# Gathered rows of experts 2 to 7: through a scratch in DRAM and VectorE's 32x32 turn, in place of transposes on TensorE

## The chip, the cores and the metric

The kernel runs on one core of one Trainium2 chip. The metric is the device time of one execution in microseconds, taken as the median of the runs.

## The reference, cut to what matters

Three stages follow each other: attention on 4 x 576 tokens with 8 heads (local or strided masks), a dense feed-forward block on 2304 tokens of 512 elements, and a mixture of 8 experts, of which each token visits two. The change is in the third stage:

```
noisy_logits = x @ w_gate + log1p(exp(x @ w_noise)) * noise
top2 = the two largest of noisy_logits, top2_w = softmax over them
out = zeros((N, D))
for e in range(E):
    for k in range(2):
        mask = top2[:, k] == e
        h = maximum(x[mask] @ w1[e], 0.0)
        out[mask] += top2_w[mask, k, None] * (h @ w2[e])
```

N is 2304, D is 512, E is 8, and the inner width is 1024. All data are float32.

## The kernel before

Rows of x, the output of the second stage, lie in DRAM in `x2d`. A list in DRAM (`lst`) holds for each expert the rows that chose it and their weights. Each expert has room for 608 rows (`CAP`), cut into five blocks of 128, 128, 128, 128 and 96 (`blk`). For an expert, `e_list` loads its list, and `e_part` gathers the rows with indirect DMAs issued by GpSimd, one a block, into `rows`, token by partition. The matmuls of the first layer need the 512 elements on partitions, so each block is turned by four transposes on TensorE into the PSUM bank `PB[7]` (line 736). From there ScalarE copies the high part and VectorE subtracts for the low part (lines 738 and 739): every float32 product is made of three reduced-precision ones, high by high, high by low and low by high. From expert 2 on, part 0 holds blocks 2 to 4 (352 rows, in `xa`) and part 1 holds blocks 0 and 1 (256 rows, in `xb`); for experts 0 and 1 part 0 holds blocks 0 to 2.

The expert's inner width is cut into 8 chunks of 128, and a slice of the main loop works on one chunk h: `m2_l1(h)` is 24 matmuls, 12 for each part, followed by a Relu on ScalarE (line 775) and a step on VectorE (line 776) for either part into `ht`; then `step()` moves the preparation of the next expert on by one yield; then `m2_l2(h - 1)` is 15 matmuls with the chunk before (lines 789 to 791), into five PSUM banks that `e_out` drains in the first slice of the next expert: multiplied by the weight into `y` and scatter-added to `out` by indirect DMAs of GpSimd (line 807).

The preparation of expert e + 1 (`e_prep`) is a generator appended in the second slice of expert e. In the kernel before, the blocks are turned in its later slices, one a slice, and the last one by `drain()` at the first slice of the new expert.

Weights are loaded ahead: `w2_load` issues two loads of 256 KB a chunk on SyncE's queue (line 669) into three `raw` buffers, ScalarE and VectorE split them (lines 677 and 678), and the result is held in a pool of 14 slots, `wp`, which `ht` and `xb` share. The gathers and `y` share four double buffers (`rap`).

TensorE's order is written out by hand. The order of the other engines and of SyncE's queue comes from a planner, which places an instruction where its model of the times has it ready. `tc.issue_after(ins)` keeps instructions behind `ins` on their engine; `LASTMM` is the last matmul of the second layer so far. The routing of the second stage turns its own rows in two ways: on TensorE with every fourth column (line 550), and for three of its chunks by a store to `x2d` (line 523), a reload in blocks of 32 (line 530) and VectorE's 32x32 turn (line 538).

Of the kernel before, what the change touches and what calls it, by code (L numbers as in the profile page):

```python
# [9 lines left out]
F32 = mybir.dt.float32  # L10
F32R = mybir.dt.float32r
# [3 lines left out]
OP = mybir.AluOpType  # L15
# [6 lines left out]
N = B * S  # L22
DM = H * D
FF = 2048
NFC = FF // 128
E = 8
F2 = 1024
NF2 = F2 // 128
# [13 lines left out]
DUMP = WIDE  # L42
# [61 lines left out]
def tile_kernel(ctx, tc, qkL, qkS, vL, vS, wm1, wm2, wgn, noise, cst, lst0, out):  # L104
    nc = tc.nc
    const = ctx.enter_context(tc.tile_pool(name="const", bufs=1))
    dram = ctx.enter_context(tc.tile_pool(name="dram", bufs=1, space=bass.MemoryType.DRAM))
    psum = ctx.enter_context(tc.tile_pool(name="psum", bufs=1, space=bass.MemoryType.PSUM))

    PB = [psum.tile([128, 512], F32, tag=f"pb{i}", name=f"pb{i}") for i in range(8)]  # L110
    x2d = dram.tile([N + DUMP, DM], F32, name="x2d")
    lst = dram.tile([E * LIST, 2], F32, name="lst")

    cs = const.tile([128, C_W], F32, name="cs")
    ident = cs[:, C_ID:C_ID + 128]
# [8 lines left out]
    with ExitStack() as main, tc.manual_schedule(engines={mybir.EngineType.PE}):  # L124
        wp = main.enter_context(tc.tile_pool(name="wp", bufs=NFC - 2))
        rap = main.enter_context(tc.tile_pool(name="rap", bufs=4))
        xtp = main.enter_context(tc.tile_pool(name="xtp", bufs=3))
# [555 lines left out]
        XE, EL = {}, {}  # L683
# [8 lines left out]
        def e_list(e, b0, b1, queue=nc.sync):  # L692
            if e not in EL:
                area = tmp.tile([128, 3 * NBLK], F32, tag="el", name="el", bufs=3)
                EL[e] = (area[:, :2 * NBLK].rearrange("p (n t) -> p n t", t=2), area[:, 2 * NBLK:].bitcast(I32))
            l, ix = EL[e]
            r0 = e * LIST
            queue.dma_start(l[:, b0:b1], lst[r0 + 128 * b0:r0 + 128 * b1, :].rearrange("(b p) t -> p b t", p=128))
            nc.gpsimd.tensor_copy(ix[:, b0:b1], l[:, b0:b1, 0])
# [10 lines left out]
        def e_part(e, part, known=N + DUMP, wait=0, gate=None):  # L710
            blocks = blocks_of(e, part)
            l, ix = EL[e]
            n = sum(map(blk, blocks))
            if part == 0:
                x = xtp.tile([128, 2, 4, n], F32R, tag="xt", name=f"xa{e}")
            else:
                x = wp.tile([128, 2, 4, n], F32R, tag="w", name=f"xb{e}")
            XE[e, part] = x
            rows = rowtiles(len(blocks), f"g{e}_{part}", known < N + DUMP)
            for i, b in enumerate(blocks):  # L720
                nc.gpsimd.indirect_dma_start(rows[i][:blk(b)], None, x2d[:known],
                                             bass.IndirectOffsetOnAxis(ap=ix[:blk(b), b:b + 1], axis=0),
                                             bounds_check=known - 1, oob_is_err=True)
            while gate is not None and not gate:
                yield
            for i, b in enumerate(blocks):
                if gate is None:
                    yield
                if not i:
                    for _ in range(wait):  # L730
                        yield
                pb = PB[7 if gate is None else 6 + i].rearrange("p (k t) -> p k t", t=128)
                m = blk(b)
                with tc.issue_after(LASTMM[0]):
                    for kc in range(4):
                        nc.tensor.transpose(pb[:, kc, :m], rows[i][:m, 128 * kc:128 * kc + 128], ident[:m, :m])  # L736
                o = slice(128 * i, 128 * i + m)
                nc.scalar.copy(x[:, 0, :, o], pb[:, :, :m])
                nc.vector.tensor_sub(x[:, 1, :, o], pb[:, :, :m], x[:, 0, :, o].bitcast(F32))
            yield  # L740

        def e_prep(e):
            if e == 1:
                e_list(e, NA // 128, NBLK)
            else:
                e_list(e, 0, NBLK)
                yield from e_part(e, 0, wait=1)
            yield from e_part(e, 1)

        HT = {}  # L750

        def m2_l1(h, parts=(0, 1), mid=None, early=False, odd=0):
            e = h // NF2
            w = W2[h]
            if not e:
                HT[h] = tmp.tile([128, 2, CH], F32R, tag="g", name=f"ht{h}")
            elif h == EARLY[-1] and early:
                HT[h] = xtp.tile([128, 2, WIDE], F32R, tag="xt", name=f"ht{h}")
            elif h not in HT:
                HT[h] = wp.tile([128, 2, WIDE], F32R, tag="w", name=f"ht{h}")  # L760
            ht = HT[h]
            for s in parts:
                x = XE[e, s]
                blocks = blocks_of(e, s)
                n = sum(map(blk, blocks))
                o = 128 * blocks[0] if e else 0
                ps = PB[(h + odd) % 2 if len(parts) == 1 else s][:, :n]
                for kc in range(4):
                    if mid and kc == 2:
                        mid()  # L770
                    a = slice(128 * kc, 128 * kc + 128)
                    nc.tensor.matmul(ps, w[:, 0, a], x[:, 0, kc, :], start=(kc == 0), stop=False)  # L772
                    nc.tensor.matmul(ps, w[:, 0, a], x[:, 1, kc, :], start=False, stop=False)  # L773
                    nc.tensor.matmul(ps, w[:, 1, a], x[:, 0, kc, :], start=False, stop=(kc == 3))  # L774
                nc.scalar.activation(ht[:, 0, o:o + n], ps, AF.Relu)  # L775
                nc.vector.scalar_tensor_tensor(ht[:, 1, o:o + n], ps, 0.0, ht[:, 0, o:o + n].bitcast(F32),  # L776
                                               op0=OP.max, op1=OP.subtract)

        def m2_l2(h, tiles=range(NBLK), mid=None):
            fc = h % NF2  # L780
# [43 lines left out]
        for c in range(3):  # L824
            xtile(c)
        parts = [groups(0, (0, 1)), locals_of(0, (2,)) + groups(1, (0,)), locals_of(1, (1, 2)),
                 groups(2, (0, 1)), locals_of(2, (2,)) + groups(3, (0,)), locals_of(3, (1, 2))]
# [10 lines left out]
        k = 0  # L838
# [50 lines left out]
        for i, (c, fc) in enumerate(seq):  # L889
# [13 lines left out]
            t, g = m1_l1(c, fc, step, conv)  # L903
# [143 lines left out]
    with tc.tile_pool(name="ovf", bufs=1) as op:  # L1047
        n = nc.values_load(nrow[:, 0:1], min_val=0, max_val=NJ)
        with tc.For_i(0, n, 1) as j:
            e8 = nc.sync.value_load(jrow[:, bass.ds(j, 1)], min_val=0, max_val=(E - 1) * NF2)  # L1050
            s0 = nc.sync.value_load(jrow[:, bass.ds(j + NJ, 1)], min_val=0, max_val=E * LIST - 128)
            l = op.tile([128, 2], F32, name="ol")
            ix = op.tile([128, 1], I32, name="oix")
            nc.sync.dma_start(l, lst[bass.ds(s0, 128), :])
            nc.vector.tensor_copy(ix, l[:, 0:1])
            r = op.tile([128, DM], F32, name="orow")
            nc.gpsimd.indirect_dma_start(r, None, x2d, bass.IndirectOffsetOnAxis(ap=ix[:, 0:1], axis=0),
                                         bounds_check=N + DUMP - 1, oob_is_err=True)
            xt = op.tile([128, 4, 128], F32, name="oxt")
            pb = PB[7].rearrange("p (k t) -> p k t", t=128)  # L1060
            for kc in range(4):
                nc.tensor.transpose(pb[:, kc], r[:, 128 * kc:128 * kc + 128], ident)
            nc.vector.tensor_copy(xt, pb)
            w = op.tile([128, NF2, 1024], F32, name="ow")
            nc.sync.dma_start(w, wm2[bass.ds(e8, NF2)].rearrange("f p n -> p f n"))
            for fc in range(NF2):
                ps = PB[fc % 2][:, :128]
                for kc in range(4):
                    nc.tensor.matmul(ps, w[:, fc, 128 * kc:128 * kc + 128], xt[:, kc], start=(kc == 0), stop=(kc == 3))
                ht = op.tile([128, 128], F32, name="oht", bufs=2)  # L1070
                nc.scalar.activation(ht, ps, AF.Relu)
                nc.tensor.matmul(PB[2], ht, w[:, fc, 512:], start=(fc == 0), stop=(fc == NF2 - 1))
            y = op.tile([128, DM], F32, name="oy")
            nc.scalar.mul(y, PB[2], l[:, 1:2])
            nc.gpsimd.indirect_dma_start(
                out, bass.IndirectOffsetOnAxis(ap=ix[:, 0:1], axis=0), y, None,
                bounds_check=N + DUMP - 1, oob_is_err=True, compute_op=OP.add)


def _layout(q, k, v, moe_w_in, moe_w_out, moe2_w_gate, moe2_w_noise, moe2_noise, moe2_w1, moe2_w2):  # L1080
    f = np.float32
# [32 lines left out]
    vz[:, :, :, :GQ] = vs.reshape(B, 2, 2, NG, GQ, D).transpose(0, 1, 3, 4, 2, 5)  # L1114
    a["vS"] = vz.reshape(B, 2, NG, 128, 2 * D)

    def stack(w1, w2, nf):
        p1 = w1.reshape(4, 128, nf, 128).transpose(2, 1, 0, 3).reshape(nf, 128, 512)
        return p1, w2.reshape(nf, 128, 512)

    w = np.concatenate(stack(moe_w_in, moe_w_out, NFC), 2)
    a["wm1"] = np.ascontiguousarray(w).view(np.int64)
    a["wm2"] = np.concatenate([np.concatenate(stack(moe2_w1[e], moe2_w2[e], NF2), 2) for e in range(E)], 0)
    g = np.concatenate([moe2_w_gate, moe2_w_noise], 1)
    a["wgn"] = g.reshape(128, 4, 2 * E)
    a["noise"] = moe2_noise.reshape(NT, 128, E).transpose(1, 0, 2)
# [18 lines left out]
```

## Time and profile before

| what | value |
|---|---|
| median of 3 runs | 987.45 us (985.74 to 989.91) |
| profiled execution | 989.13 us, of which the span is 987.3 |
| granted TensorE clock, mean of the span | 0.992 |
| TensorE matmul busy | 963.9 us, 98% |
| VectorE busy | 496.2 us, 50% |
| ScalarE busy | 384.8 us, 39% |
| GpSimd busy | 218.7 us, 22% |

The profile is one execution. A line number is that of the kernel listed above. "PE" is TensorE's matmuls, "PEld" its weight loads, "DVE" VectorE, "ACT" ScalarE, "POOL" GpSimd, "SPq" SyncE's queue; a q behind a name is the engine's sequencer. Matmuls are pipelined: the duration of one is longer than the distance from its start to the next start, and it is the distance that adds up.

### The profile page before, as it was taken

The page shows a single profiled execution, that of the slowest core. Times are in us where ns is not written, and L with a number is a line of the kernel's source. Part 1 is how long each engine was busy: PE and PEld are TensorE (multiplying, and loading weights), DVE is VectorE, ACT ScalarE, POOL GpSimd, SP SyncE. Part 2 cuts the span into 40 slices and gives each one's busy share as a digit, 9 for nine tenths or more (in the row PEclk, how much of TensorE's full clock was granted, in tenths as well). Part 3 has the DMA queues.
Part 4 walks back from the last instruction along what each step waited for, and adds up shares of the span by engine and source line. Part 5 has one row for each costly group of instructions (what it writes and reads, how often), then busy time and mean ns, then how long its engine had stood idle before and what let it go on. Part 6 is the DMA issues. An engine that isn't in the chain of part 4 may idle for free.

```text
span 987.3 us, 16175 instructions
## 1 busy us (share of the span) xinstructions
PE 963.9 (98%) x5798; PEld 854.2 (87%) x5798; DVE 496.2 (50%) x1528; ACT 384.8 (39%) x1071; POOL 218.7 (22%) x206
## 2 busy tenths in 40 slices
PE   6899999999999999999999999999999999999996
PEld 5778899898888889898889988989898989898995
DVE  6779965467645745623666342333433343343410
ACT  6665543244444444223354242333333333242311
POOL 3565321020200100020230502050503204050303
PEclk9799999999999999999999999999999999999999
DMA  9835522052323237301153344171634427272403
GB/s 297 301 123 174 198 70 72 1 102 75 54 91 109 66 68 243 116 2 65 25 189 118 57 147 107 64 187 65 155 97 106 145 86 166 75 177 86 84 1 51
DMA packets 68193, 108.99 MB, mean 110 GB/s; under 512 B 12672, under 2 KB 30720, under 8 KB 68096
## 3 DMA queue, kind: packets, MB, share of 16 engines
q1 hardware_dynamic: 58288, 87.97, 28.8%
q0 software_dynamic: 9824, 19.98, 10.7%
q8 instruction: 46, 0.75, 0.3%
q14 instruction: 35, 0.29, 0.1%
HBM read 85.86 MB, written 22.21 MB: 109 GB/s over the span
## 4 chain that ended last, share of the span: by engine, by line
PE 87%; issue 5%; DVE 4%; ACT 1%; POOL 1%; DMA 1%; SPq 0%; POOLq 0%; ACTq 0%; DVEq 0%
PE pb L463 7%; PE pb L487 6%; PE pb L774 6%; PE pb L789 6%; PE pb L791 6%; PE pb L772 6%; PE pb L773 6%; PE pb L465 6%; PE pb L464 6%; PE pb L790 6%; PE pb L489 6%; PE pb L488 6%; PE pb L736 2%; PE pb L219 2%; PE pb L234 1%
## 5 line engine op out<-in xcount | busy, mean ns | idle before, releaser
L776 DVE SCALAR_TENSOR_TENSOR ht<-pb,ht 128x256 fp32r<-128x256 f32 (+3 forms) x128 | 60.4, 472 | 235.9 <-ACT ht L775 233.2
L775 ACT ACTIVATE ht<-pb 128x256 fp32r<-128x256 f32 (+3 forms) x128 | 54.3, 424 | 248.2 <-PE pb L774 236.5
L463 PE MATMUL pb<-xt,w 128*128 128x384 f32 x384 | 132.2, 344 | 0.0
L465 PE MATMUL pb<-xt,w 128*128 128x384 f32 x384 | 130.3, 339 | 0.0
L807 POOL DMA_INDIRECT out<-y,el x40 | 63.2, 1579 | 301.6 <-ACT y L806 270.6
L464 PE MATMUL pb<-xt,w 128*128 128x384 f32 x384 | 129.8, 338 | 0.0
L789 PE MATMUL pb<-w,ht 128*128 128x512 f32 (+1 forms) x320 | 128.1, 400 | 0.0
L791 PE MATMUL pb<-w,ht 128*128 128x512 f32 (+1 forms) x320 | 125.6, 393 | 0.1
L790 PE MATMUL pb<-w,ht 128*128 128x512 f32 (+1 forms) x320 | 125.2, 391 | 0.0
L487 PE MATMUL pb<-w,g 128*128 128x512 f32 x288 | 118.1, 410 | 0.1
L489 PE MATMUL pb<-w,g 128*128 128x512 f32 x288 | 113.6, 395 | 0.0
L488 PE MATMUL pb<-w,g 128*128 128x512 f32 x288 | 113.1, 393 | 0.0
L653 POOL DMA_INDIRECT lst<-pay,si x36 | 35.9, 997 | 325.2 <-DVE si L650 285.7
L470 DVE SCALAR_TENSOR_TENSOR th<-th,pb 128x384 f32<-128x384 f32 x96 | 52.8, 550 | 106.9 <-ACT th L468 104.2
L468 ACT ACTIVATE th<-pb 128x384 f32<-128x384 f32 x96 | 47.0, 490 | 127.7 <-PE pb L465 112.3
L678 DVE TENSOR_TENSOR w<-raw,w 128x512 fp32r<-128x512 f32 x128 | 84.1, 689 | 16.3 <-ACT w L677 15.7
L772 PE MATMUL pb<-xa,w 128*128 128x352 f32 (+1 forms) x256 | 84.5, 330 | 0.0
L774 PE MATMUL pb<-xa,w 128*128 128x352 f32 (+1 forms) x256 | 83.6, 326 | 0.0
L773 PE MATMUL pb<-xa,w 128*128 128x352 f32 (+1 forms) x256 | 83.1, 325 | 0.0
L677 ACT CAST w<-raw 128x512 fp32r<-128x512 f32 x128 | 74.3, 618 | 14.5 <-DMA raw<-wm 12.4
L463 PEld LDWEIGHTS pb<-xt,w 128*128 128x128 f32 x384 | 72.6, 189 | 4.9 <-issue 1.0
L464 PEld LDWEIGHTS pb<-xt,w 128*128 128x128 f32 x384 | 72.6, 189 | 3.9 <-DVE xt L206 0.2
(180 smaller groups left out, 1906.2 us busy)
## 6 DMA issues: line engine op xcount, KB each, us to landing
raw<-wm SPq DMA_DIRECT2D x136, 256.0 KB
area<-wm SPq DMA_DIRECT2D x28, 512.0 KB
out<-zero SPq DMA_DIRECT2D x7, 768.0 KB
qk<-qkL SPq DMA_DIRECT2D x16, 304.0 KB
att<-qkS SPq DMA_DIRECT2D x20, 189.0 KB
qk<-qkS SPq DMA_DIRECT2D x20, 189.0 KB
v<-vL SPq DMA_DIRECT2D x16, 192.0 KB
att<-qkL SPq DMA_DIRECT2D x8, 304.0 KB
```

Of the source, the lines that this page charges most:

```text
L463: nc.tensor.matmul(ps, w[0][:, a], X[c][:, 0, kc, :], start=(kc == 0), stop=False)
L464: nc.tensor.matmul(ps, w[0][:, a], X[c][:, 1, kc, :], start=False, stop=False)
L465: nc.tensor.matmul(ps, w[1][:, a], X[c][:, 0, kc, :], start=False, stop=(kc == 3))
L487: nc.tensor.matmul(o, g[:, 0, a], w[0], start=((c, fc) in FIRST), stop=False)
L488: nc.tensor.matmul(o, g[:, 0, a], w[1], start=False, stop=False)
L489: m = nc.tensor.matmul(o, g[:, 1, a], w[0], start=False, stop=((c, fc) in LAST))
L772: nc.tensor.matmul(ps, w[:, 0, a], x[:, 0, kc, :], start=(kc == 0), stop=False)
L773: nc.tensor.matmul(ps, w[:, 0, a], x[:, 1, kc, :], start=False, stop=False)
L774: nc.tensor.matmul(ps, w[:, 1, a], x[:, 0, kc, :], start=False, stop=(kc == 3))
L789: nc.tensor.matmul(o, g[:, 0, a], w[:, 0, 512:], start=(fc == 0), stop=False)
L790: nc.tensor.matmul(o, g[:, 0, a], w[:, 1, 512:], start=False, stop=False)
L791: m = nc.tensor.matmul(o, g[:, 1, a], w[:, 0, 512:], start=False, stop=(fc == NF2 - 1))
```

## The change

From expert 2 on, `e_turn` takes the place of `e_part`. In the first slice all five blocks are gathered. In the second, part 0's rows are stored to a scratch in DRAM, `xs`, and loaded back by four DMAs, each of which brings a quarter of the elements to 32 partitions, for all tokens; in the third the same is done for part 1. In slices four to seven VectorE's transpose turns one block at a time (two in the sixth) into `PB[7]`, in 32x32 squares, behind the last step of line 776; ScalarE's copy and VectorE's subtraction follow as before. With this layout an element's partition is its index divided by four, so the rows of the first layer's weights are permuted to match on the host, and the transposes that remain on TensorE (experts 0 and 1, and the overflow loop at the end) take every fourth column.

```diff
+    xs = dram.tile([2, 640, DM], F32, name="xs")
...
                     for kc in range(4):
-                        nc.tensor.transpose(pb[:, kc, :m], rows[i][:m, 128 * kc:128 * kc + 128], ident[:m, :m])
+                        nc.tensor.transpose(pb[:, kc, :m], rows[i][:m, kc::4], ident[:m, :m])
...
+        def e_turn(e):
+            l, ix = EL[e]
+            parts = []
+            for part in range(2):
+                blocks = blocks_of(e, part)
+                n = sum(map(blk, blocks))
+                if part == 0:
+                    x = xtp.tile([128, 2, 4, n], F32R, tag="xt", name=f"xa{e}")
+                else:
+                    x = wp.tile([128, 2, 4, n], F32R, tag="w", name=f"xb{e}")
+                XE[e, part] = x
+                rows = rowtiles(len(blocks), f"g{e}_{part}")
+                for i, b in enumerate(blocks):
+                    nc.gpsimd.indirect_dma_start(rows[i][:blk(b)], None, x2d,
+                                                 bass.IndirectOffsetOnAxis(ap=ix[:blk(b), b:b + 1], axis=0),
+                                                 bounds_check=N + DUMP - 1, oob_is_err=True)
+                parts.append((x, rows, blocks))
+            yield
+            todo = []
+            for part, (x, rows, blocks) in enumerate(parts):
+                if part:
+                    yield
+                n = sum(map(blk, blocks))
+                mem = xs[e % 2, 384 * part:384 * part + n, :]
+                for i, b in enumerate(blocks):
+                    nc.sync.dma_start(mem[128 * i:128 * i + blk(b), :], rows[i][:blk(b)])
+                tr = wp.tile([128, 4 * n], F32, tag="w", name=f"tr{e}")
+                for a in range(4):
+                    nc.sync.dma_start(tr[32 * a:32 * a + 32, :].rearrange("p (b d) -> p b d", d=128),
+                                      mem[:, 128 * a:128 * a + 128].rearrange("(b i) d -> i b d", i=32))
+                for i, b in enumerate(blocks):
+                    m = blk(b)
+                    todo.append((x, tr[:, 512 * i:512 * i + 4 * m], i, m))
+            for j, (x, tr, i, m) in enumerate(todo):
+                if j != 3:
+                    yield
+                pb = PB[7][:, :4 * m]
+                with tc.issue_after(LASTHT[0]):
+                    nc.vector.transpose(pb, tr.rearrange("p (b i k) -> p b k i", k=4, i=32))
+                pb = pb.rearrange("p (b k i) -> p k b i", k=4, i=32)
+                hi, lo = (x[:, j, :, 128 * i:128 * i + m].rearrange("p k (b i) -> p k b i", i=32) for j in range(2))
+                nc.scalar.copy(hi, pb)
+                nc.vector.tensor_sub(lo, pb, hi.bitcast(F32))
+            yield
+
         def e_prep(e):
             if e == 1:
                 e_list(e, NA // 128, NBLK)
+                yield from e_part(e, 1)
             else:
                 e_list(e, 0, NBLK)
-                yield from e_part(e, 0, wait=1)
-            yield from e_part(e, 1)
+                yield from e_turn(e)
...
-                nc.vector.scalar_tensor_tensor(ht[:, 1, o:o + n], ps, 0.0, ht[:, 0, o:o + n].bitcast(F32),
-                                               op0=OP.max, op1=OP.subtract)
+                low = nc.vector.scalar_tensor_tensor(ht[:, 1, o:o + n], ps, 0.0, ht[:, 0, o:o + n].bitcast(F32),
+                                                     op0=OP.max, op1=OP.subtract)
+            LASTHT[0] = low.ins
...
-                nc.tensor.transpose(pb[:, kc], r[:, 128 * kc:128 * kc + 128], ident)
+                nc.tensor.transpose(pb[:, kc], r[:, kc::4], ident)
...
+        if turned:
+            w1 = w1.reshape(128, 4, nf * 128).transpose(1, 0, 2)
```

## Rows read from the trace of the kernel before

**Rows 1.** The page's first part: busy us, share of the span, instructions.

```profile
PE 963.9 (98%) x5798; PEld 854.2 (87%) x5798; DVE 496.2 (50%) x1528; ACT 384.8 (39%) x1071; POOL 218.7 (22%) x206
```

**Rows 2.** Stretches: us, busy us by engine (and instructions), granted clock, DMA share, GB/s.

```profile
207.00:223.20 16.20, 16.20 (x115) 14.64 (x114) 10.48 (x46) 7.91 (x29) 1.21 (x2) 1.00 0.78 164
...
642.74:699.28 56.54, 56.54 (x334) 50.82 (x333) 21.89 (x40) 19.31 (x40) 13.33 (x11) 1.00 0.46 119
```

**Rows 3.** The timeline of POOL: start, length, instruction, idle before it.

```profile
642.74 1.63 POOL L807 DMA_INDIRECT out<-y,el  x1 [39.56 <-ACT y L806]
...
699.28 1.63 POOL L807 DMA_INDIRECT out<-y,el  x1 [38.72 <-ACT y L806]
```

**Rows 4.** Waits of PEld from 560 to 960: us in total, times, longest.

```profile
PEld pb L791 <- DVE ht L776: 0.9, 2, 0.5
PEld pb L789 <- ACT ht L775: 0.3, 1, 0.3
PEld pb L736 <- DVE xb L739: 0.3, 1, 0.3
```

**Rows 5.** The chain that ended last: start, length, piece.

```profile
651.05 0.23 PE pb L791
...
657.85 0.23 PE pb L791
...
665.09 0.23 PE pb L791
...
675.92 0.33 PE pb L736 x4
```

**Rows 6.** Lines 736 and 550 (ns min/median/max), and TensorE's timeline around line 550.

```profile
L736 PEld LDWEIGHTS pb<-cs,g x160: 138/140/143, 508.8 to 920.0; 128*128 128x128 f32 x128, 96*128 96x128 f32 x32
...
L550 PEld LDWEIGHTS pb<-cs,row x12: 196/206/212, 452.5 to 458.1; 128*128 128x128 f32 x12
...
452.69 0.63 PE L550 MATMUL pb<-cs,row 128*128 128x128 f32 x4
...
453.39 0.40 PE L488 MATMUL pb<-w,g 128*128 128x512 f32 x1
453.63 0.40 PE L489 MATMUL pb<-w,g 128*128 128x512 f32 x1
```

**Rows 7.** Line 538 (ns min/median/max), and groups by form (busy us, mean ns).

```profile
L538 DVE STREAM_TRANSPOSE x2t<-row x6: 1057/1090/1103, 308.2 to 396.7; 128x512 f32<-128x512 f32 x6
...
L678 DVE TENSOR_TENSOR w<-raw,w 128x512 fp32r<-128x512 f32 x106 | 69.5, 689 | 11.1 <-ACT w L677 10.6 <-issue 0.4
...
L739 DVE TENSOR_TENSOR xb<-pb,xb 128x512 fp32r<-128x512 f32 x14 | 9.7, 692 | 15.0 <-ACT xb L738 15.0
L738 ACT CAST xb<-pb 128x512 fp32r<-128x512 f32 x14 | 8.2, 587 | 15.4 <-PE pb L736 13.6 <-PE pb L791 1.5
```

**Rows 8.** Timelines of VectorE, POOL and TensorE over one slice's end and the next.

```profile
648.66 0.42 DVE L776 SCALAR_TENSOR_TENSOR ht<-pb,ht 128x256 fp32r<-128x256 f32 x1
...
652.22 1.09 POOL L721 DMA_INDIRECT g<-x2d,el  x1 [0.30 <-issue]
...
653.05 0.28 PE L772 MATMUL pb<-xb,w 128*128 128x256 f32 x1
...
653.74 0.53 DVE L776 SCALAR_TENSOR_TENSOR ht<-pb,ht 128x352 fp32r<-128x352 f32 x1 [4.66 <-ACT ht L775]
```

**Rows 9.** Lines 523 and 530 (ns min/median/max), and SyncE's wait from 200 to 240.

```profile
L523 SPq DMA_DIRECT2D x2d<-part x3: 320/326/326, 207.9 to 209.1; - x3
...
L530 SPq DMA_DIRECT2D part<-x2d x12: 323/430/447, 216.1 to 222.2; - x12
...
SPq L530 <- DMA x2d<-part: 6.1, 1, 6.1
```

**Rows 10.** Waits of SyncE's queue and of ScalarE, 600 to 950: total, times, longest.

```profile
SPq L698 <- DMA out<-y,el: 23.4, 4, 7.7
...
ACT w L677 <- DMA raw<-wm: 3.0, 5, 1.3
```

More of the change, by code (lines that the diff above doesn't have):

```diff
@@ L744, in e_prep @@
                 e_list(e, NA // 128, NBLK)
+                yield from e_part(e, 1)
             else:
                 e_list(e, 0, NBLK)
-                yield from e_part(e, 0, wait=1)
-            yield from e_part(e, 1)
+                yield from e_turn(e)
         HT = {}
+        LASTHT = [None]
         def m2_l1(h, parts=(0, 1), mid=None, early=False, odd=0):
@@ L1115, in _layout, with stack @@
     a["vS"] = vz.reshape(B, 2, NG, 128, 2 * D)
-    def stack(w1, w2, nf):
+    def stack(w1, w2, nf, turned=False):
+        if turned:
+            w1 = w1.reshape(128, 4, nf * 128).transpose(1, 0, 2)
         p1 = w1.reshape(4, 128, nf, 128).transpose(2, 1, 0, 3).reshape(nf, 128, 512)
@@ L1122, in _layout @@
     a["wm1"] = np.ascontiguousarray(w).view(np.int64)
-    a["wm2"] = np.concatenate([np.concatenate(stack(moe2_w1[e], moe2_w2[e], NF2), 2) for e in range(E)], 0)
+    a["wm2"] = np.concatenate([np.concatenate(stack(moe2_w1[e], moe2_w2[e], NF2, True), 2) for e in range(E)], 0)
     g = np.concatenate([moe2_w_gate, moe2_w_noise], 1)
```

## The prediction

> **What bounds the kernel now.** I read the page's busy times first: TensorE is busy 98% of the span, VectorE 50%, ScalarE 39% [rows 1]. Then whole expert periods, cut from the first scatter-add of one expert to that of the next [rows 2, 3] (one stands there, three more are like it): TensorE is busy 56.54 of 56.54 us, VectorE 21.9, ScalarE 19.3, at a granted clock of 1.00 (the 2.4 GHz level). The waits of TensorE's weight loads over the 400 us of the expert stage come to 1.5 us in all [rows 4]. So in this stage every instruction on TensorE is path, and only its pitch counts; the others' idle time is free until it makes TensorE wait.
>
> What a group of four transposes (one block of rows) adds is read from the chain [rows 5]: the last matmul of a slice ends a step at 651.05 and 657.85 in a slice without transposes (6.80 us), at 657.85 and 665.09 with a 128-row block (7.24). A 128-row block costs 0.44. The 96-row block has the rest of the period: 56.54 - 8 x 6.80 - 4 x 0.44 = 0.38; its own row in the chain shows 0.33 [rows 5], and the matmul behind it some more.
>
> **The change part by part.**
>
> *Removed:* experts 2 to 7 lose five groups of transposes each, 4 of 128 rows and one of 96: 6 x (4 x 0.44 + 0.38) = 12.8 us of TensorE time; nothing else of the stage's matmuls changes.
>
> *Kept but changed:* ten blocks of experts 0 and 1 are still transposed on TensorE, now with every fourth column. The routing does this in line 550: its weight loads take 206 to 209 ns against 140 in line 736 [rows 6]. Its group begins at 452.69 and the second matmul behind it at 453.39: 0.70 us, of which a matmul alone takes 0.24 (453.39 to 453.63), so 0.46 a group, 0.02 to 0.03 more than 0.44. Ten groups: 0.3 us. If the longer loads weren't hidden it would be 40 x 0.069 = 2.8; the nearest row is the group's own pitch, so 0.3. That the weights' rows are permuted to match is host layout: the same bytes in the same loads.
>
> *Added on VectorE:* five turns an expert. The trace has them SBUF to SBUF: 1.09 us for 128x512 [rows 7]; the 96-row one by its elements 0.82. The target is now PSUM, which no transpose of before writes; a subtraction that reads PSUM (line 739) takes 0.69 us, one from SBUF (line 678) 0.69 [rows 7], so I take 1.09, with 2.2 as the upper end (double) and 0.53 as the lower (the 128x352 step of line 776 [rows 8]). ScalarE's copy (0.59) and VectorE's subtraction (0.69) of a block exist already; they read the bank in another order, which I take at nothing. VectorE's load goes from 21.9 to 27.1 us of a 54.4 us period. What hides it: in a slice VectorE ends its last step at 649.08 and starts the next slice's first at 653.74 [rows 8], 4.66 us idle. A 128-row block needs 1.09 + 0.59 + 0.69 = 2.37. The sixth slice holds two blocks through one PSUM bank, 1.85 + 2.37 = 4.2: just inside. If it overran, the next slice's first step would end late (654.27 here), but its bank is wanted again only behind the last matmul at 657.85 [rows 5], 3.8 us later, so a few tenths cost nothing. The last block, in the seventh slice, would end at 649.08 + 2.37 = 651.45 on this clock; part 1's first matmul of the next expert corresponds to 653.05. Margin 1.6, cost 0; with the 2.2 us turn still 0.5.
>
> *Added on SyncE's queue and the DMA engines:* per expert five stores and eight loads. Issues cost 0.33 and 0.43 us in lines 523 and 530 [rows 9], so 5.1 us of issuing per period: hidden. Bytes: 608 rows x 2 KB twice is 2.5 MB; at 119 GB/s the share is 0.46 [rows 2], so 46 GB/s more makes it about 0.64. The stretch with the routing's own store and reload ran at 0.78 and TensorE stayed full [rows 2], so bandwidth is not the bound.
>
> The wait is the open cost. The queue is in order. A store waits for its gather, the loads wait for the stores to land, and behind both stand the weight loads (line 669). Their casts stand on ScalarE between the two Relus of a slice, so a late weight load delays the second Relu, then the step that frees the bank of part 1; that step ends at 649.08 and TensorE wants the bank at 653.05 [rows 8], a slack of 3.97 us. The gathers are issued from 652.22 on [rows 8], five in a row as after the change too, so POOL's own queue keeps its order; the stores come after them. Expert 2's rows go through in slices of expert 1 that compute only part 1, and have the least time. For one store-to-load hop the only row is 6.1 us [rows 9]. Of such a hold this slack covers the most, and the casts' own margin comes on top: the queue is held already for 7.7 us once an expert by the index list (line 698), and casts waited 1.3 us at the longest [rows 10] and TensorE 0.5 [rows 4]. Two holds an expert (parts 0 and 1 go in different slices). Lower end 0, since loads are not needed for five slices and the cover above absorbs a hold; upper end (6.1 - 3.97) = 2.1 us a hold, 25 us in all. The nearest row, the 7.7 us hold that cost TensorE next to nothing, says near 0; I allow as much again as TensorE waits today, 1.5 us [rows 4].
>
> The Trainium skill (SBUF — State Buffer, "The DMA setup-cost knee") gives a fixed 2 us per transfer plus bytes over 436 GB/s. An estimate from it for a 0.7 MB hop is 3.7 us, under the slack, and the sum would lose its 1.5; no run here shows a lone hop, and the one row is longer.
>
> *The slots:* reloaded rows take two more of the 14 slots of the weight pool, and xb is claimed earlier. Seven weights, two ht, two xb and two tr make 13: no wait. Rows leave their gather buffers earlier.
>
> **Sum.** The profiled execution took 989.13 us (span 987.3 and 1.8 around it). 989.13 - 12.8 + 0.3 + 1.5 = 978.1. It lay 1.7 above the median of the three runs, 987.45, so I predict 976.4 for the median.
>
> **Rivals.**
>
> *One hold an expert reaches TensorE.* For it: the hop of 6.1 us, and the stores of part 0 come just after the scatter-adds, when the queue is held anyway. Against: [rows 10]. Six stalls of 2.1 instead of the 1.5: 976.4 - 1.5 + 12.6 = 987.5, no change. Chance 0.16.
>
> *Both holds reach it.* 25.2 instead of 1.5: 1000, slower. Break-even is (12.8 - 0.3) / 6 = 2.1 us an expert, so it decides when each of the two holds the queue more than 5.0 us (3.97 and half of 2.1). Chance 0.10. Against it speaks that part 1's store comes a slice later, when its gathers have long landed.
>
> *VectorE becomes the path.* If every turn delayed TensorE by its own length, 24 x 1.09 + 6 x 0.82 = 31 us would be given back: 976.4 - 1.5 + 31 = 1006. It needs slices in which VectorE has less than a block's time idle; [rows 8] shows 4.66 against 4.2. Chance 0.05. The Trainium skill (VectorE: DVE Perf Modes, "Rules for kernel authors") says to transpose 128x128 on TensorE if PSUM may be the target, which speaks for the kernel before. By duration this trace agrees (0.44 against 1.09), but the 0.44 is path and the 1.09 lies beside it.
>
> *The forecast:* 0.69, with its own range of 972.5 (no waits, and the 2 us by which the runs scatter) to 982.5 (waits of 1 us an expert, loads unhidden).
>
> **How the numbers follow.** A run of this kernel scatters by about 2 us, so 0.5%, 4.9 us, is about what can be told from no change: 982.5 and 992.4 are the bounds. Faster: the forecast and some of the first rival, 0.72. Same: the rest of that rival and of the second where only some stalls come, 0.15. Slower: 0.13. The range goes from 972.5 to 990, which takes in most of the first rival and leaves out 0.18.
>
> **What would show it.** The step between experts' first scatter-adds falls from 56.5 to 54.4 us; every slice is 6.80; line 736 has 40 transposes; TensorE stays at full busy in the expert stage. The turns read 1.1 us and lie in VectorE's idle stretch after the second ht step. Holds show as ScalarE's cast waiting for raw by more than 4 us, followed by TensorE weight loads waiting for ht. The prediction is wrong if slices at an expert's second and third step grow longer than 6.80 us, if the sixth or the first slice does (VectorE), or if experts 0 and 1 lose more than a microsecond to line 736.

## The result and the profile after

The changed kernel takes 978.41 us (median of 6 runs, 974.97 to 981.5), the kernel before 987.92 us (6 runs beside them). The ratio is 0.9899, with an interval of 0.9881 to 0.9918: 9.5 us or 1.0% faster. The forecast was 976.4 us, 2.0 us too low.

The page's first part of the changed kernel answers to [rows 1]:

```profile
PE 947.5 (97%) x5678; PEld 839.5 (86%) x5678; DVE 528.9 (54%) x1558; ACT 387.8 (40%) x1071; POOL 216.6 (22%) x206
```

TensorE has 120 matmuls fewer and 16.4 us less busy time (4.1 of them ahead of the mark in the first stage that is used below: 89.8 us busy up to it before, 85.7 after); VectorE has 30 instructions and 32.7 us more. What this is worth shows in an expert's period. The first fence is POOL's timeline with the first scatter-adds of three experts, the second the stretch between the first two, with columns as in [rows 2]:

```profile
639.24 1.63 POOL L857 DMA_INDIRECT out<-y,el  x1 [40.29 <-ACT y L856]
...
693.65 1.64 POOL L857 DMA_INDIRECT out<-y,el  x1 [29.73 <-ACT y L856]
...
748.05 1.63 POOL L857 DMA_INDIRECT out<-y,el  x1 [30.20 <-ACT y L856]
```

```profile
639.24:693.65 54.41, 54.41 (x314) 48.79 (x313) 27.06 (x45) 19.87 (x40) 13.32 (x12) 1.00 0.66 168
```

The period is 54.41 and 54.40 us, against 56.54 [rows 2, 3]: all of the 2.13 us of a set of five groups is gone, and TensorE is still busy to the last hundredth, now with 314 matmuls instead of 334. VectorE went from 21.9 to 27.1 us a period and the DMA share from 0.46 to 0.66.

TensorE's remaining waits in the expert stage, to be held against [rows 4], are these (total, times, longest; sequencer's weight loads, then matmuls):

```profile
PEld pb L821 <- DVE ht L825: 1.0, 1, 1.0
PEld pb L822 <- DVE xb L787: 0.3, 1, 0.3
...
PE pb L821 <- DVE ht L825: 0.7, 1, 0.7
```

There is one stall of note in the whole stage, 1.0 us at the weight load (the 0.7 of the matmul is the same stall seen behind it; the expectations below add the two, which counts it twice). The chain through 598 to 612 us shows where it comes from, in expert 1:

```profile
600.64 0.50 ACT ht L824
...
601.34 5.12 DMA raw<-wm
...
606.48 0.63 ACT w L678
...
607.13 0.29 DVE w L679
...
607.74 0.40 DVE ht L825
```

A load of weights (line 670 now) goes out at 601.34, between the loads of the two parts of expert 2's detour (599.32 and 603.75), and takes 5.12 us to land, where 3.0 is the median of all. ScalarE's cast, which stands ahead of the second Relu, is ready for it from 601.64 on and waits until 606.48, and TensorE for the bank that the ht step then frees. So the detour did reach TensorE through a late load, once in the kernel and not once an expert. From 640 to 960 us neither matmuls nor weight loads wait at all.

The detour's own waits in SyncE's queue (590 to 950 us; line 770 is a store, 773 a reload) are nearly all for gathers, not for the landing of the stores:

```profile
SPq L770 <- DMA g<-x2d,el: 62.3, 25, 9.5
...
SPq L773 <- DMA xs<-g: 1.4, 3, 0.5
```

**Where the rest of the difference lies.** The two profiled executions differ by 14.2 us (989.13 and 974.97), more than the medians. Part of that lies ahead of anything that was changed. The first tanh of ScalarE after 100 us is the same instruction in both (before, then after):

```profile
103.49 0.48 ACT L468 ACTIVATE th<-pb 128x384 f32<-128x384 f32 x1
```

```profile
100.92 0.48 ACT L469 ACTIVATE th<-pb 128x384 f32<-128x384 f32 x1
```

From this mark to the end it is 987.3 - 103.49 = 883.8 us before and 973.2 - 100.92 = 872.3 after, 11.5 less. Of that, five periods give 5 x 2.13 = 10.65, and the stretch from expert 0's first scatter-add to expert 1's 83.68 - 82.44 = 1.2 (642.74 less 559.06 before; 639.24 less 556.80 now), where the whole set would have been 2.1 (four of the ten strided groups lie in it). From the mark to that stretch it is 0.3 longer, with the other six strided groups in it. Spans from this mark are used below beside the medians, since they leave out a part that no edit touches.

### The profile page after: what moved, and what is told of

The parts are those of the page before. It is cut to its first block, busy times and chain, and to the rows that moved or that the text cites. A ratio compares the mean times of both kernels' runs of the same rounds, so it can differ in the third digit from the quotient of the medians.

```text
span 973.2 us, 16018 instructions
## 1 busy us (share of the span) xinstructions
PE 947.5 (97%) x5678; PEld 839.5 (86%) x5678; DVE 528.9 (54%) x1558; ACT 387.8 (40%) x1071; POOL 216.6 (22%) x206
## 4 chain that ended last, share of the span: by engine, by line
PE 83%; DVE 6%; issue 5%; ACT 3%; DMA 2%; POOL 1%; SPq 0%; POOLq 0%; ACTq 0%; DVEq 0%
PE pb L488 6%; PE pb L464 6%; PE pb L823 6%; PE pb L490 6%; PE pb L821 6%; PE pb L822 6%; PE pb L466 6%; PE pb L489 6%; PE pb L465 6%; PE pb L839 6%; PE pb L841 6%; PE pb L840 6%; PE pb L220 1%; PE pb L235 1%; PE pb L265 1%
```

## The experiments

| kernel | median, us | ratio to before, interval | from the mark to the end, us |
|---|---|---|---|
| before | 987.9 to 988.7 | | 883.8 |
| changed | 978.41 | 0.9899 (0.9881 to 0.9918) | 872.3 |
| changed, again | 978.66 | 0.9894 (0.9877 to 0.9911) | 873.1 |
| groups twice | 1002.02 | 1.0137 (1.0116 to 1.0158) | 896.0 |
| layout alone | 990.35 | 1.0022 (1.0009 to 1.0035) | 886.9 |
| detour alone, two blocks in a slice | 997.70 | 1.0087 (1.0070 to 1.0105) | 893.4 |
| detour alone, one block a slice | 990.01 | 1.0014 (1.0004 to 1.0024) | 885.4 |
| changed without detour | 977.85 | 0.9891 (0.9874 to 0.9909) | 872.3 |
| detour twice | 1017.20 | 1.0286 (1.0270 to 1.0302) | 909.7 |
| turns twice | 990.07 | 1.0014 (1.0005 to 1.0022) | 884.6 |
| turns twice, last block earlier | 976.13 | 0.9869 (0.9852 to 0.9885) | 873.9 |
| expert 2 a slice later | 976.71 | 0.9876 (0.9859 to 0.9892) | 871.6 |
| expert 1 too | 977.67 | 0.9891 (0.9874 to 0.9907) | 871.3 |
| both | 976.99 | 0.9899 (0.9881 to 0.9917) | 870.3 |

Each ratio is to the kernel before, run again beside the variant. A time from the mark is that of one profiled execution, and two of the changed kernel differ by 0.8 us.

The theory was the prediction's: a group is worth its pitch on TensorE (P), and the detour costs what its holds push onto TensorE. The rivals were that the gain comes in part from elsewhere (H), and that the holds cost more than the profile shows.

**Groups twice.** The kernel before, each group of experts 2 to 7 done twice.

```diff
-                    for kc in range(4):
+                    for kc in [0, 1, 2, 3] * (2 if e > 1 else 1):
                         nc.tensor.transpose(...)
```

> The kernel before, in which experts 2 to 7 do each group of four transposes twice (30 more groups). Theory P (a group costs its pitch on TensorE, 0.44 us, and nothing else): 30 groups add 12.8 us, 987.9 becomes 1000.7, ratio 1.013; an expert's period goes from 56.5 to 58.7. Rival H (a group's worth is not its pitch, and a part of the 9.5 us that the medians show, or of the 14 us between the two profiled executions, comes from elsewhere): the doubling adds clearly less or more, under 8 or over 17 us.

The median rose by 13.4 us, the time from the mark by 12.2; a period is 702.73 to 761.32, 58.59, so 2.05 more than 56.54, where the removal gave 2.13. The price of a group is its pitch, in either direction.

**Layout alone.** The changed kernel with `e_part` for all experts.

```diff
-                yield from e_turn(e)
+                yield from e_part(e, 0, wait=1)
+                yield from e_part(e, 1)
```

> The changed layout alone: weights permuted, every transpose still on TensorE but with every fourth column, nothing through DRAM. Theory P (the longer weight loads of a strided transpose are hidden but for 0.02 to 0.03 us a group): 40 groups add 1.0 us, 988.9, ratio 1.001. Rival (the loads' 0.069 us each is not hidden): 160 x 0.069 = 11 us, 999, ratio 1.011.

Between the two, nearer to P: the period is 698.32 to 755.16, 56.84, 0.30 more for five groups, 0.06 a group where the prediction had 0.025. An estimate from this for the ten groups of the changed kernel is 0.6 us instead of 0.3; by the time from the mark, 3.1 us for forty groups, it would be 0.8.

**Detour alone.** The kernel before with the stores and loads of `e_turn`, but nothing reads `tr`, and TensorE transposes the gathered rows.

```diff
+                tr = wp.tile([128, 4 * n], F32, tag="w", name=f"tr{e}")
+                for a in range(4):
+                    nc.sync.dma_start(tr[32 * a:32 * a + 32, :]..., mem[:, 128 * a:128 * a + 128]...)
...
+            for j, (x, r, i, m) in enumerate(todo):
+                if j != 3:
+                    yield
+                pb = PB[7].rearrange("p (k t) -> p k t", t=128)
+                with tc.issue_after(LASTMM[0]):
+                    for kc in range(4):
+                        nc.tensor.transpose(pb[:, kc, :m], r[:m, 128 * kc:128 * kc + 128], ident[:m, :m])
```

> The kernel before plus the detour alone: all five blocks gathered in the first slice, stored and loaded back in the second and third, but nothing reads what comes back; the transposes stay on TensorE in slices four to seven. Theory P (holds of the queue cost TensorE only the 1.7 us stall that the changed kernel's profile shows in expert 1): 987.9 + 1.7 = 989.6, ratio 1.002, with casts waiting for raw as in the changed kernel. Rival H (the 3 us by which the medians fall short of 12.5 are holds that other executions pay): 991 or more, ratio 1.003 or more; the rival of the prediction (one hold an expert reaches TensorE): 1000, ratio 1.013.

It took 9 us more, and not for a reason that either theory had. TensorE's waits in this run:

```profile
PE pb L781 <- DVE xa L784: 7.0, 6, 1.2
PE pb L817 <- DVE ht L821: 1.3, 1, 1.3
```

The first is my arrangement: two groups in the sixth slice share one bank, and the second waits for VectorE to have read the first, six times. The run told nothing of the detour, so it was repeated with one block a slice (`yield` for every j; the last block at the start of the next expert, as before).

> As the run with the detour alone, but with one block a slice on TensorE (the last one at the start of the next expert, as in the kernel before), since there two groups in one slice waited for the one PSUM bank, 1.2 us an expert. Theory P (the detour costs TensorE only the stall in expert 1): period 56.5 as before, 988.4 + 1.7 = 990, ratio 1.002. Rival H (holds reach TensorE in every expert): period over 57, 991.5 or more.

That came out at 990.01 with 990 expected, with a period of 700.25 to 756.78, 56.53, exactly that of the kernel before. SyncE's queue waits for gathers for 63.7 us in this run, up to 9.1 at a time, and TensorE has one stall, in expert 1, where the stretch between scatter-adds is 85.08 instead of 83.68:

```profile
PE pb L816 <- DVE ht L820: 1.6, 1, 1.6
...
ACT w L678 <- DMA raw<-wm: 26.6, 13, 5.7
```

**Changed without detour.** VectorE turns the gathered rows as they lie, so the first layer gets other operands; the last block is gathered with 128 rows.

```diff
-                    nc.sync.dma_start(mem[...], rows[i][:blk(b)])
...
-                    todo.append((x, tr[:, 512 * i:512 * i + 4 * m], i, m))
+                    todo.append((x, rows[i][:, :4 * m], i, m))
```

> The changed kernel without the detour: VectorE turns the gathered rows as they lie (so 32x32 squares stay where they are and the first layer of experts 2 to 7 gets other operands), and the last block is gathered with 128 rows. Theory P: the stall of 1.7 us in expert 1 goes, 978.4 - 1.7 = 976.7, ratio to before 0.9887, and casts no longer wait for raw by more than 2 us. Rival H: 975.4 or less, ratio 0.987 or less. If the period of 54.4 us itself falls, the detour costs more than its stalls.

It is 0.6 us below the changed kernel by the median, above what either theory expected, and level with it from the mark. Casts still wait for raw, by up to 2.9 us. The stretch from expert 0's first scatter-add to expert 1's is 82.42 us here and 82.44 in the changed kernel (83.3 in its second profile, below), and TensorE's weight loads wait 2.0 us in it against 1.8, in several short waits instead of one longer one. So what the detour's 13 transfers an expert cost, from 0 to 0.9 us by the profiles, is at the limit of what these runs resolve, and the 0.9 us by which the stretch falls short of the 2.1 is lacking without the detour too.

**Detour twice.** Every store and load of the changed kernel done a second time.

```diff
+                for _ in range(2):
                     for i, b in enumerate(blocks):
                         nc.sync.dma_start(mem[...], rows[i][:blk(b)])
                     for a in range(4):
                         nc.sync.dma_start(tr[...], mem[...])
```

> The changed kernel with every store and every load of the detour done twice, the second store behind the first loads. Each hop lands in about 4 us in the changed kernel's profile, so SyncE's queue is held some 8 us more a part, on top of the 9 us for which the first store waits for its gather. Theory S (slack: the queue may be held until casts come about 4 us late on ScalarE; more goes to TensorE): if the planner leaves weight loads behind the second hop, 8 - 4 = 4 us a part or more, an expert's period grows from 54.4 by 2 to 8 us, 990 to 1030. Rival O (what protects TensorE is the order that the planner gives, which puts the casts behind the longer hops too): period 54.4, 978 to 982.

The time is 39 us above the changed kernel's, with periods of 61.2 to 63.4 us. So there is an edge, and this crosses it. The waits of VectorE (640 to 950) and of TensorE, VectorE's timeline, and two stretches (columns as in [rows 2]):

```profile
DVE pb L784 <- DMA tr<-xs: 46.2, 5, 9.8
...
PE pb L822 <- DVE ht L826: 25.0, 6, 6.4
```

```profile
665.61 0.42 DVE L826 SCALAR_TENSOR_TENSOR ht<-pb,ht 128x256 fp32r<-128x256 f32 x1 [0.82 <-ACT ht L825]
675.33 1.09 DVE L784 STREAM_TRANSPOSE pb<-tr 128x512 f32<-128x512 f32 x1 [9.29 <-DMA tr<-xs]
...
681.25 0.52 DVE L826 SCALAR_TENSOR_TENSOR ht<-pb,ht 128x352 fp32r<-128x352 f32 x1
```

```profile
639.66:703.09 63.43, 57.01 (x314) 51.01 (x313) 27.22 (x45) 19.73 (x40) 13.33 (x12) 0.95 0.70 184
682.00:684.00 2.00, 2.00 (x7) 2.00 (x8) 1.71 (x3) 0.25 (x1) 0.00 (x0) 0.50 0.66 182
```

Theory S had nearly the size (2 to 8 us an expert, where 6.8 to 9.0 came) but the wrong door. The casts do not wait longest; the first turn does. In the changed kernel VectorE's turns wait for the reload too, 3.3 us in four waits from 640 to 911 us, at most 1.1. So the reload, whose arrival the prediction did not price, lands as it is wanted, and what protects TensorE is that the bank of the next ht step is wanted 3.8 us later. Nine microseconds are beyond that.

The waits are not all of the 37.4 us from the mark. Behind a wait of 6.4 us that ended at 681.83 TensorE's granted clock is 0.50 (the 1.2 GHz level), and the mean of the five periods is 0.94 to 0.95, where the changed kernel has 1.00. With the same 314 matmuls a period TensorE is busy 12.6 us longer over the five. So a late reload was paid for twice here, by the wait and by the slower matmuls behind it.

**Turns twice.** The changed kernel, VectorE's transpose issued twice a block.

```diff
                 with tc.issue_after(LASTHT[0]):
-                    nc.vector.transpose(pb, ...)
+                    for _ in range(TURNS):
+                        nc.vector.transpose(pb, ...)
...
+TURNS = 2
```

> The changed kernel with every turn done twice on VectorE. Theory P (the turns lie in idle time; the sixth slice would need 6.2 us of 4.7 idle, and the next slice's bank is wanted 3.8 us later): period 54.4 to 54.9 by the hand-over of the last block, 978 to 981.5. Rival V (VectorE is at its margin, each further turn is path): 24 x 1.09 + 6 x 0.86 = 31 us, 1009, period 59.7.

Neither: 990.07 us, 11.6 more than the changed kernel, periods of 55.70 (756.33 to 812.03). TensorE's waits:

```profile
PE pb L823 <- ACT xb L788: 5.2, 6, 2.8
PE pb L824 <- DVE xb L789: 2.1, 6, 0.3
```

Six times, once an expert, the first matmuls on xb wait for the last block. Expert 1 pays most: the stretch between its scatter-adds is 87.66 us instead of 82.44, the period behind it 56.48, and the later ones are some 1.3 us longer than in the changed kernel. The prediction left that hand-over a margin of 0.5 us for a turn of 2.2. VectorE's timeline of this run, over the sixth and the seventh slice, shows what it overlooked:

```profile
682.88 0.53 DVE L827 SCALAR_TENSOR_TENSOR ht<-pb,ht 128x352 fp32r<-128x352 f32 x1 [1.01 <-ACT ht L826]
...
684.57 1.77 DVE L785 STREAM_TRANSPOSE pb<-tr 128x384 f32<-128x384 f32 x2
...
687.47 2.25 DVE L785 STREAM_TRANSPOSE pb<-tr 128x512 f32<-128x512 f32 x2
690.71 0.69 DVE L789 TENSOR_TENSOR xb<-pb,xb 128x512 fp32r<-128x512 f32 x1 [0.99 <-ACT xb L788]
691.32 1.28 DVE L680 TENSOR_TENSOR w<-raw,w 128x512 fp32r<-128x512 f32 x2
692.52 0.85 DVE L827 SCALAR_TENSOR_TENSOR ht<-pb,ht 128x352 fp32r<-128x352 f32 x2
693.28 1.09 DVE L785 STREAM_TRANSPOSE pb<-tr 128x512 f32<-128x512 f32 x1
694.28 0.67 DVE L680 TENSOR_TENSOR w<-raw,w 128x512 fp32r<-128x512 f32 x1
694.87 1.08 DVE L785 STREAM_TRANSPOSE pb<-tr 128x512 f32<-128x512 f32 x1
695.86 0.67 DVE L680 TENSOR_TENSOR w<-raw,w 128x512 fp32r<-128x512 f32 x1
696.60 0.69 DVE L789 TENSOR_TENSOR xb<-pb,xb 128x512 fp32r<-128x512 f32 x1
```

The two blocks of the sixth slice run over its end (684.57 to 691.4), and the ht steps of the seventh come 9.6 us after those of the sixth instead of 6.8. That alone TensorE doesn't feel, as the prediction had it; but it pushes the last block, whose turn and subtraction have weight splits between them as well, past the start of the next expert. If the hand-over is the margin, the same doubled turns must cost nothing when the last block comes a slice earlier:

```diff
-                if j != 3:
+                if j not in (2, 4):
                     yield
```

> Every turn twice, as before, but the two-block slices are the fifth and the sixth and none is left for the seventh. The doubled turns cost 11.6 us in the last arrangement, 1.3 us an expert period, where the first matmuls on xb waited for the last block. Theory Y (the hand-over of the last block to the next expert is the margin): with the last block a slice earlier the period returns to 54.4 and the time to about 980. Rival V (VectorE's queue is full: two doubled blocks in a slice delay the ht steps and through them the banks): the period stays above 55.2, 986 or more.

They do, within what the runs resolve: 976.13 us with 60 turns instead of 30, and periods of 54.40 from 749.92 on (54.6 in the two before). From the mark it is 1.6 and 0.8 us longer than the two profiles of the changed kernel, most of it in expert 1, where a stall of 1.6 us stands (line 823 on ht). Theory Y holds: two-block slices overrun here too, but the seventh slice takes it up, and VectorE as a whole is not full.

**Expert 2 a slice later.**

```diff
             yield
+            if e == 2:
+                yield
             todo = []
...
-                if j != 3:
+                if j != 3 and not (e == 2 and j == 1):
```

> The changed kernel with expert 2's detour one slice later (stores from the third slice of expert 1 on instead of the second, turns of its five blocks in slices five to seven). Theory S (what is left of TensorE's waiting in the changed kernel is one stall of 1.7 to 2.8 us in expert 1, where a weight cast waits 4.8 to 5.4 us for its load behind expert 2's stores and loads, in slices that compute only part 1): the stall goes, 978.5 - 2 = 976.5, ratio to before 0.988. Rival O (the queue's hold only moves): the same stall stands a slice later, 978.5.

The median is 976.71 as expected, and TensorE's stall in expert 1 is gone. What is left there:

```profile
PE pb L824 <- DVE xb L789: 0.2, 1, 0.2
```

From the mark to the end it saves 0.7 us against the first profile of the changed kernel and 1.5 against the second. The medians' intervals overlap, so the gain itself is not resolved.

**Expert 1 too.** Its part 0 is stored in the third slice of expert 0 and turned in the sixth to eighth; its part 1 goes through the following slices.

```diff
-                pre1 = e_part(1, 0, N + DUMP - CH)
+                pre1 = e_one(0, N + DUMP - CH, 1, 0)
...
-            if 2 <= h < 6:
+            if h in (2, 5, 6, 7):
                 next(pre1, None)
```

Here `e_one` is `e_turn` for one part, with the yields given. 

> The changed kernel with expert 1's five blocks sent the same way too (part 0 stored in the third slice of expert 0 and turned in the sixth to eighth; part 1 through the slices of expert 0's second part). Theory P (each group of strided transposes is worth 0.5 us of TensorE): 5 x 0.5 = 2.5 us less, 976. Rival (these slices compute 384 or 224 columns only and are 2.6 to 4.3 us long, so holds and turns have no cover): 978.5 or more.

And with both edits:

> The two last edits together: expert 1's blocks go through the scratch too, and expert 2's detour is a slice later. Theory S and P together: the stall of 2.0 to 2.5 us in expert 1, which stood in either kernel without the later slice, goes, and five groups of 0.5 us leave TensorE: 978.5 - 2 - 2.5 = 974, ratio to before 0.985. Rival (the short slices of expert 0 have no cover): 976.5 or more, with TensorE waiting in the stretch ahead of expert 1 or in it.

By the medians neither differs from the changed kernel (977.67, between the two expectations, and 976.99, on the rival's side). From the mark they are 1.0 and 2.0 us shorter than its first profile, and both have a stall that it lacks, between 556 and 600 us, in the short slices of the end of expert 0 and the start of expert 1, as the rival had it (this is the one with both edits):

```profile
PE pb L879 <- ACT ht L864: 1.9, 1, 1.9
```

**Changed, again.**

> The changed kernel once more, to see in another execution where it stands. Theory P: from the first scatter-add to the end it is 11.8 us shorter than the kernel before in every execution (period 54.4), and what the medians lack to that lies ahead of the first scatter-add, in the stage whose granted clock differs from run to run. Rival H: a period or expert 1 is longer than in the first profile, by the 2 us that are lacking.

The period is 54.40 again (694.55 to 748.95) and the mark stands at 101.05. From the mark it is 873.1 us, 10.8 less than before; the stall in expert 1 was 1.6 us this time, and the stretch between its scatter-adds 83.3 instead of 82.4:

```profile
PEld pb L821 <- DVE ht L825: 1.6, 1, 1.6
...
PE pb L821 <- DVE ht L825: 1.2, 1, 1.2
```

So H found no longer period, but its other place, expert 1, is 0.9 us longer, and from the first scatter-add to the end it is 11.0 us shorter than the kernel before, not 11.8. The longer stall goes with that and is the larger part of what varies between the two.

## Why the prediction was right, point by point

- **TensorE's pitch as the price (12.8 us).** Right: 2.13 us a period in five periods, 12.2 to 13.4 us for the same groups added. Expert 1, where the sixth set lay, shows 1.2 of its 2.1, with the detour and without it; four strided groups, 0.2 by the price below, are a part of what lacks there, and the rest stays open.
- **Strided transposes (0.3 us).** Mis-sized: 0.06 us a group, 0.6 for ten. The nearest row counted only two matmuls behind one group; the weight loads of line 737 read 210 ns (median), as expected:

```profile
L737 PEld LDWEIGHTS pb<-cs,g x40: 196/210/223, 506.4 to 570.8; 128*128 128x128 f32 x32, 96*128 96x128 f32 x8
```

- **The turn into PSUM (1.09 and 0.82 us).** Right: 1.09 and 0.86 in the rows. It costs nothing that shows, but the margin at the hand-over was put too high: a doubled turn was to leave 0.5 us and cost 1.3 a period, and more in expert 1.

```profile
L783 DVE STREAM_TRANSPOSE pb<-tr 128x512 f32<-128x512 f32 x24 | 26.3, 1094 | 3.5 <-DMA tr<-xs 3.3
...
L783 DVE STREAM_TRANSPOSE pb<-tr 128x384 f32<-128x384 f32 x6 | 5.2, 863 | 0.0
```

- **Holds of SyncE's queue (1.5 us, up to 25).** The size was near, in part by luck: the 1.5 was an allowance as large as today's waits, not the price of a hold. The hold was also another than the one priced. The prediction took 6.1 us a hold for the landing of the stores; the reloads waited for that 1.4 us in all, and the queue stood for the gathers instead, some 10 us an expert and up to 9.5 at a time. (The 7.7 us in [rows 10], "once an expert", was the longest of four waits that come to 23.4.) TensorE doesn't feel it from expert 2 on. Expert 1, whose slices the prediction named as having the least time, has the one stall, 1.0 to 1.6 us, behind a weight load that went out only as it was wanted and took 2.1 us longer than the median to land. The sign that the prediction named for a hold, a cast waiting more than 4 us and weight loads waiting for ht behind it, came there and nowhere else (4.8 us). Against the run without the detour this costs 0 to 0.9 us. That the loads "are not needed for five slices" was true of the weights and not of the reload: its turn already waits for it.
- **DMA load (share 0.64).** 0.66, and no period shows it as a bound. The one late load of expert 1 came while the detour's own transfers were under way.
- **The slots of the weight pool (no wait).** Not tried alone; the full periods of 54.4 us leave no room for a wait that reaches TensorE.
- **The rival of the Trainium skill** (VectorE: DVE Perf Modes, "Rules for kernel authors": transposes of 128x128 belong on TensorE if PSUM will do). Not borne out here: 1.09 us beside the path replaced 0.44 on it. The doubled detour and the doubled turns show where that cover ends.
- **The two microseconds between forecast and median.** From the profiles 10.8 to 11.5 us were gained after the mark against 11.0 forecast; the medians show 9.5 and 10.0. What executions lose or win ahead of the mark covers the difference in size, but that this is the cause was not shown. Two terms of the sum were off and went some way to cancel: the strided groups were put 0.3 too low, the holds 0.6 to 1.5 too high.
- **The range.** The terms named for the forecast's own range give 972.9 to 983.4 (976.4 less 1.5 and 2; 976.4 and 4.5 and 2.5), not 972.5 to 982.5. Nothing hangs on it.

## What to carry to other kernels

Where an engine is busy in every hundredth of a stage, an instruction taken from it is worth its pitch, and work put beside it is free up to a margin that sits at particular places: here the first turn's reload and the last block's hand-over. Look for that place by doubling the added work, since the busy shares (VectorE 27 of 54 us) don't show it. Beyond the margin the price can be more than the wait, as the slower matmuls behind the doubled detour's stalls show. Then move the step at the margin: the doubled turns went from 11.6 us by the medians to nothing that the runs resolve when one block moved by one slice.

## What was not expected of the hardware

The mark in the first stage stood at 100.7 to 101.5 us in eight profiled executions of these kernels and at 102.9 to 103.9 in six, the kernel before among the latter, though no edit touches what lies ahead of it. The granted clock of the first 37 us was 1.00 in the profile of the changed kernel and 0.91 in that of the kernel before, but 0.91 too in its second execution with the mark at 101.05, so that clock alone doesn't explain it. It goes along in part: it is 0.87 to 0.91 in all six late ones and 0.91 to 1.00 in the eight others. At 2.6 us it is as large as a quarter of the effect, and it stays open.

The stores of the detour took 4.0 us (median) from issue to landing and the loads 3.7 to 4.3, at 256 and 128 to 176 KB. The prediction's estimate by the Trainium skill (SBUF — State Buffer, "The DMA setup-cost knee") for a hop of part 0 was 3.7 us; it put a store and a load of 0.7 MB down as one transfer. Here one store, a third of those bytes, takes longer than that, beside the gathers and weight loads, and a whole hop, store and load, is by an estimate from the two medians nearer 8.
